# A chunked scan with a feed-forward layer: output sums of the middle blocks moved, two loads on another queue, the last product in another bank

## The chip, the cores and the metric

The kernel runs on one core of one Trainium2 chip. The metric is the device time of one execution in microseconds (us). The page of a profile calls the engines PE (TensorE, matmuls), PEld (its weight loads), DVE (VectorE), ACT (ScalarE), POOL (GpSimd) and SP (SyncE). A name with a q (ACTq, SPq) is the engine's instruction queue: DMA issues and waits, not arithmetic. L372 is line 372 of the kernel.

The kernel before has two levels of time, some 5 us apart, and which one a run takes changes from run to run. Runs of the upper level are called slow. Where a kernel's runs all lie close together they are all counted as fast, even if their clock is low.

## The reference, cut to what matters

```python
# x (4, 8, 768, 32), a (4, 8, 768), B and C (4, 8, 768, 16), float32
# a scan with decays over the sequence, per head
cum = np.cumsum(log_a, axis=-1)
L = np.exp(cum[:, :, :, None] - cum[:, :, None, :]) * causal
y_intra = (C B^T * L) @ x
y_inter = (C @ state) * exp(cum)
state = decay_full * state + sum(B x * decay_from_j)
# a feed-forward layer on its output: 3072 tokens of 256, hidden 768
h = np.maximum(np.maximum(y @ w1, y @ w2), y @ w3)
out = h @ w_out
```

(The einsums are abbreviated.) The kernel cuts the sequence into six chunks of 128 tokens (NC = 6) instead of 32, takes four batches and eight heads at once, and does the feed-forward products with seven block products instead of eight (that is why there are so many sums and quarters in it).

## The kernel before: the parts that matter here

Loads and their queue. Every load below is issued by SyncE (`nc.sync`):

```python
    def load(c, name):                         # L122: B, C or x of chunk c
        ...
        nc.sync.dma_start(out=t, in_=src[:, :, c * P:(c + 1) * P, :].rearrange(...))

    def decay_load(c, pairs=(0, 2)):           # L369: two loads of 1 MB, decays of chunk c
        L = decays(c) if 0 in pairs else Ls[c]
        for b in pairs:
            nc.sync.dma_start(out=L[:, b:b + 2]..., in_=cums[...].partition_broadcast(P))

    def last_load(c):                          # L377: eight small loads (32 KB each), "E"
        for h in range(NH):
            nc.sync.dma_start(out=E[h * N:(h + 1) * N], in_=rows[h].partition_broadcast(N))
```

One step of the feed-forward part. ScalarE's copy L653 opens a chain that frees the PSUM banks for TensorE: L653 on ScalarE, L654 to L656 on VectorE, then products of the next step.

```python
    def early(c, k):                           # L628 are the products
        products(c, k, [(1, A, 0), (6, A, 1), (5, B, 0), (7, B, 1)], True)
        ...
        nc.scalar.copy(out=eu[:, 0], in_=A[:, 0])                                      # L653
        nc.vector.tensor_tensor(out=eu[:, 1], in0=A[:, 1], in1=eu[:, 0], op=ALU.add)   # L654
        nc.vector.tensor_tensor(out=v, in0=B[:, 1], in1=eu[:, 1], op=ALU.add)          # L655
        nc.vector.tensor_tensor(out=t[:, 2], in0=B[:, 0], in1=v, op=ALU.add)           # L656

    def quarter_sums(o, t):                    # of the output; L745, L746, L747
        nc.vector.tensor_tensor(out=t[:, 0], in0=o[:, 1], in1=t[:, 1], op=ALU.add)
        nc.vector.tensor_tensor(out=t[:, 2], in0=o[:, 3], in1=t[:, 0], op=ALU.add)
        nc.vector.tensor_tensor(out=t[:, 3], in0=o[:, 2], in1=t[:, 2], op=ALU.add)
```

The loop interleaves, in block c, the feed-forward part of chunk c, the scan of chunk c + 1 and the output of chunk c - 1. Lists say what goes with which of nine steps: X and Y which piece (scores "s0", "s2", scan "y", output product "D"), P how many waiting VectorE instructions are popped at three points of a step. `flush()` issues the quarter sums that wait.

```python
    for c in range(1, NC):
        n = c + 1
        for k in range(NW):                    # nine steps
            early(c, k)
            ...                                # pieces of X; pops
            maximum = late(c, k)
            if n < NC and k == 0:
                loads(c + 2)                   # all loads of chunk c + 2
            ...
            pop(ps_[k][2])                     # score weightings (L491), sums of y (L553)
            flush()                            # quarter sums (L745 to L747)
            later[:0] = maximum
            ...
```

## Time and profile before

| | before |
|---|---|
| four runs, us | 297.81, 297.83, 302.54, 303.39 |
| profiled run (slow) | 302.34, span 300.6, mean granted TensorE clock 0.988 |
| TensorE busy | 94% of the span |
| waits that the change is aimed at | 7.3 us in all, counted in the prediction |

### The profile page before, as it was taken

The page shows a single profiled execution, that of the slowest core. Times are in us where ns is not written, and L with a number is a line of the kernel's source. Part 1 is how long each engine was busy: PE and PEld are TensorE (multiplying, and loading weights), DVE is VectorE, ACT ScalarE, POOL GpSimd, SP SyncE. Part 2 cuts the span into 40 slices and gives each one's busy share as a digit, 9 for nine tenths or more (in the row PEclk, how much of TensorE's full clock was granted, in tenths as well). Part 3 has the DMA queues.
Part 4 walks back from the last instruction along what each step waited for, and adds up shares of the span by engine and source line. Part 5 has one row for each costly group of instructions (what it writes and reads, how often), then busy time and mean ns, then how long its engine had stood idle before and what let it go on. Part 6 is the DMA issues. An engine that isn't in the chain of part 4 may idle for free.

```text
span 300.6 us, 5773 instructions
## 1 busy us (share of the span) xinstructions
PE 282.3 (94%) x2204; PEld 225.9 (75%) x2204; DVE 212.9 (71%) x427; ACT 119.5 (40%) x323; POOL 112.8 (38%) x132
## 2 busy tenths in 40 slices
PE   6789999989999999899999999999989999999994
PEld 4556445478887878688977878888878888988984
DVE  2763878957789467868577868676778676677681
ACT  2946487743756345424426242525220201011101
POOL 5252656477990917900005920003530303030300
PEclk9969999999999999999999999999999999999999
DMA  7979879969787039950007690001001001000103
GB/s 90 227 248 320 181 132 178 255 173 206 210 96 106 2 96 250 106 77 2 2 0 219 145 139 27 3 0 37 0 0 37 2 1 35 2 1 0 37 0 105
DMA packets 105035, 28.15 MB, mean 94 GB/s; under 512 B 75312, under 2 KB 101936, under 8 KB 105008
## 3 DMA queue, kind: packets, MB, share of 16 engines
q1 hardware_dynamic: 104560, 27.53, 45.7%
q8 instruction: 17, 0.28, 0.4%
q10 hardware_dynamic: 448, 0.26, 0.3%
q14 instruction: 10, 0.08, 0.1%
HBM read 24.54 MB, written 3.24 MB: 92 GB/s over the span
## 4 chain that ended last, share of the span: by engine, by line
PE 77%; DVE 12%; issue 3%; DMA 3%; SPq 2%; ACT 1%; POOL 0%; DVEq 0%; ACTq 0%; POOLq 0%
PE sumB L628 22%; PE sumA L628 17%; PE o L738 15%; PE up L578 8%; PE s L483 4%; PE y L519 3%; DMA raw_x<-in_x_dram 3%; PE o L814 3%; DVE L L491 2%; PE y L506 2%; PE up L570 2%; DVE m L673 2%; PE y L530 1%; DVE rb L670 1%; SPq L125 1%
## 5 line engine op out<-in xcount | busy, mean ns | idle before, releaser
L628 PE MATMUL sumA<-yT,w 128*128 128x256 f32 x180 | 55.5, 390 | 1.4 <-DVE h L669 1.4
L653 ACT COPY eu<-sumA 128x256 f32<-128x256 f32 x45 | 16.8, 373 | 87.6 <-PE sumA L628 80.0
L391 ACT ACTIVATE L<-L,ncums 128x128 f32<-128x128 f32 x160 | 50.2, 392 | 2.5 <-POOL L L384 2.5
L628 PE MATMUL sumB<-rb 128*128 128x256 f32 x180 | 46.2, 379 | 0.0
L628 PEld LDWEIGHTS sumB<-rb 128*128 128x128 f32 x180 | 34.2, 190 | 4.7
L628 PEld LDWEIGHTS sumA<-yT,w 128*128 128x128 f32 x180 | 29.8, 190 | 9.0 <-DVE h L669 2.6
L654 DVE TENSOR_TENSOR eu<-sumA,eu 128x256 f32<-128x256 f32 x45 | 18.9, 420 | 18.9 <-ACT eu L653 18.5
L491 DVE TENSOR_TENSOR L<-s,L 128x512 f32<-128x512 f32 x46 | 29.8, 680 | 1.1 <-PE s L483 0.7
L578 PE MATMUL up<-yT,w 128*128 128x512 f32 x64 | 29.1, 600 | 0.2 <-DVE w L188 0.2
L670 DVE TENSOR_TENSOR rb<-sumB,eu 128x512 f32<-128x512 f32 x30 | 20.7, 690 | 10.4 <-PE sumB L628 10.3
L628 PE MATMUL sumB<-yT,rb 128*128 128x256 f32 x90 | 27.5, 387 | 0.6 <-DVE m L656 0.6
L185 POOL TENSOR_TENSOR w_u<-w_u,w_r 128x512 uint32<-128x512 uint32 x12 | 15.3, 1274 | 31.9 <-DVE w_u L179 15.5
L628 PE MATMUL sumB<-rb,w 128*128 128x256 f32 x90 | 26.8, 379 | 0.0
L628 PE MATMUL sumA<-rb 128*128 128x256 f32 x90 | 26.8, 379 | 0.0
L384 POOL TENSOR_SCALAR_AFFINE_SELECT L<-L 128x1024 f32<-128x1024 f32 x20 | 24.1, 1235 | 0.0
L470 POOL TENSOR_TENSOR S<-S,old 128x256 f32<-128x256 f32 x4 | 2.9, 726 | 56.2 <-DVE S L462 56.1
L713 POOL TENSOR_TENSOR L<-h 128x256 f32<-128x256 f32 x5 | 3.6, 726 | 52.2 <-DVE h L673 40.1
L655 DVE TENSOR_TENSOR v<-sumB,eu 128x256 f32<-128x256 f32 x45 | 19.1, 425 | 5.0 <-DVE eu L654 0.5
L578 PEld LDWEIGHTS up<-yT,w 128*128 128x128 f32 x64 | 11.6, 190 | 14.7 <-issue 11.7
L738 PE MATMUL o<-wo,h 128*128 128x128 f32 x120 | 17.5, 279 | 4.9 <-DVE ob L747 4.9
L738 PEld LDWEIGHTS o<-wo,h 128*128 128x128 f32 x120 | 15.9, 191 | 7.9 <-issue 5.0
L670 DVE TENSOR_TENSOR m<-sumB,eu 128x512 f32<-128x512 f32 x15 | 10.3, 690 | 15.4 <-PE sumB L628 15.3
(141 smaller groups left out, 512.5 us busy)
## 6 DMA issues: line engine op xcount, KB each, us to landing
L<-cums SPq DMA_DIRECT2D x10, 1024.0 KB, 8.8
rb<-in_moe_w_dram SPq DMA_DIRECT2D x9, 512.0 KB, 7.6
raw_x<-in_x_dram SPq DMA_DIRECT2D x6, 512.0 KB, 7.8
out_dram<-ob SPq DMA_DIRECT2D x11, 256.0 KB, 2.2
raw_B<-in_B_dram SPq DMA_DIRECT2D x6, 256.0 KB, 4.5
raw_C<-in_C_dram SPq DMA_DIRECT2D x6, 256.0 KB, 6.5
rb<-in_moe_w_out_dram SPq DMA_DIRECT2D x3, 512.0 KB, 6.0
E<-cums SPq DMA_DIRECT2D x40, 32.0 KB, 4.4
```

What stands on the lines that cost most here:

```text
L185: nc.gpsimd.tensor_tensor(out=u, in0=u, in1=r, op=ALU.add)
L384: nc.gpsimd.affine_select(out=Ls[c][:, b], in_=Ls[c][:, b], pattern=[[0, NH], [1, P]], compare_op=ALU.is_ge, fill=MASKED, base=0, channel_ ...
L391: nc.scalar.activation(L[:, b, h], L[:, b, h], AF.Exp, bias=ncum[c][:, b * NH + h:b * NH + h + 1], scale=1.0)
L483: nc.tensor.matmul(out=s[:, i].rearrange("j g i -> j (g i)"), lhsT=st["BT"][rows, b], rhs=st["CT"][rows, b].rearrange("p g i -> p (g i)"), ...
L491: nc.vector.tensor_tensor(out=M, in0=s, in1=M, op=ALU.mult)
L578: nc.tensor.matmul(out=bank, lhsT=w_sb[i][:, k, f * P:(f + 1) * P], rhs=yT[0][:, k], start=(k == 0), stop=(k == KD - 1))
L628: nc.tensor.matmul(out=bank[:, half], lhsT=left(p, k), rhs=sides[c][p], start=(first and half == 0), stop=True, skip_group_check=True)
L653: nc.scalar.copy(out=eu[:, 0], in_=A[:, 0])
L654: nc.vector.tensor_tensor(out=eu[:, 1], in0=A[:, 1], in1=eu[:, 0], op=ALU.add)
L655: nc.vector.tensor_tensor(out=v, in0=B[:, 1], in1=eu[:, 1], op=ALU.add)
L670: nc.vector.tensor_tensor(out=t[:, 0:2], in0=B, in1=eu[:, 1:2].to_broadcast([P, 2, HB]), op=ALU.add)
L738: nc.tensor.matmul(out=o[:, PLACES[p]], lhsT=token_sums[c][p][:, f, u], rhs=wo_of(p)[:, f], start=(p == 1 and f == 0), stop=True, skip_gro ...
```

## The change

Its intent: give the quarter sums a whole step before the products that need them; spread the VectorE work of block 1; let the last product start without waiting for a bank; and take two loads of chunk 2 (x, and the second half of the decays) off SyncE's queue, issuing them from ScalarE somewhat nearer to their use. The diff, cut to its core:

```diff
# part 1, block 1: VectorE's instructions popped at other points
-    P1 = [..., (1, 1, 3), (1, 1, 0), (1, 0, 0), (9, 0, 0)]
+    P1 = [..., (1, 1, 2), (1, 1, 1), (1, 0, 2), (1, 0, 2)]
# parts 2 and 3, middle blocks: scores and y one step earlier, products and quarter sums later
-    X2 = ["t", "s0", "D", "D", "s2", "D", "y", "D", "D"]
+    X2 = ["t", "s0", "D", "s2", "D", "y", "D", "D", "D"]
-    P2 = [(1, 0, 1), (1, 1, 1), (1, 0, 2), (1, 0, 0), (1, 1, 1), (1, 0, 2), (1, 0, 2), (1, 0, 2), ...]
+    P2 = [(1, 0, 1), (1, 1, 3), (0, 0, 1), (1, 1, 2), (1, 0, 0), (1, 0, 0), (9, 0, 0), (1, 0, 0), ...]
-            flush()
+            if not (1 < c < NC - 1 and k == 2):
+                flush()
# part 4, the end: last product in its own bank, ScalarE's copy and store ahead of the last sum
-        token_products(c, 1, o, (4,))
+        o = att_bank([P, 4, P], "o")
+        token_products(c, 1, o, (4,), first=4)
# part 5, the queues
-            decay_load(2, (2,))                # both stood in SyncE's list before block 1
-            load(2, "x")
+    decay_load(2, (2,), nc.scalar)             # just before block 1
+            if c == 1 and k == 1:              # in block 1, step 1
+                load(2, "x", nc.scalar)
# [helpers with a queue as an argument, and the place of a sum in the last output: cut]
```

More of the change, by code (lines that the diff above doesn't have):

```diff
@@ L120, with load @@
     sources = {"B": (B, N), "C": (C, N), "x": (x, D)}
-    def load(c, name):
+    def load(c, name, eng=nc.sync):
         src, w = sources[name]
         t = blocks[c][name] = raw.tile([P, BH, w], FP32, tag="raw_" + name, name="raw_" + name)
-        nc.sync.dma_start(
+        eng.dma_start(
             out=t, in_=src[:, :, c * P:(c + 1) * P, :].rearrange("b h s n -> s (b h) n"))
@@ L367, with decay_load @@
     cums = dram.tile([BH, NC, P], FP32, name="cums")
-    def decay_load(c, pairs=(0, 2)):
+    def decay_load(c, pairs=(0, 2), eng=nc.sync):
         L = decays(c) if 0 in pairs else Ls[c]
         for b in pairs:
-            nc.sync.dma_start(
+            eng.dma_start(
                 out=L[:, b:b + 2].rearrange("j b h i -> j (b h) i"),
@@ L733, in flush, with token_products @@
             behind.pop(0)()
-    def token_products(c, u, o, which, fs=range(NQ)):
+    def token_products(c, u, o, which, fs=range(NQ), first=1):
         for p in which:
@@ L739, in token_products, with quarter_sums @@
                     out=o[:, PLACES[p]], lhsT=token_sums[c][p][:, f, u], rhs=wo_of(p)[:, f],
-                    start=(p == 1 and f == 0), stop=True, skip_group_check=True)
-    def quarter_sums(o, t):
-        nc.vector.tensor_tensor(out=t[:, 0], in0=o[:, 1], in1=t[:, 1], op=ALU.add)
-        nc.vector.tensor_tensor(out=t[:, 2], in0=o[:, 3], in1=t[:, 0], op=ALU.add)
+                    start=(p == first and f == 0), stop=True, skip_group_check=True)
+    def quarter_sums(o, t, w):
+        nc.vector.tensor_tensor(out=w, in0=o[:, 1], in1=t[:, 1], op=ALU.add)
+        nc.vector.tensor_tensor(out=t[:, 2], in0=o[:, 3], in1=w, op=ALU.add)
         nc.vector.tensor_tensor(out=t[:, 3], in0=o[:, 2], in1=t[:, 2], op=ALU.add)
@@ L750, in new_quarters @@
         if tag == "m":
-            ob = ffn.tile([P, 4, HB], FP32, tag="m", name="m")[:, 0:2]
+            ob = ffn.tile([P, 4, HB], FP32, tag="m", name="m")
         else:
@@ L773, in output_products @@
             nc.scalar.copy(out=t[:, 1], in_=o[:, 0])
-            behind.append(lambda: quarter_sums(o, t))
+            behind.append(lambda: quarter_sums(o, t, t[:, 0]))
         if 4 in which:
@@ L846, in last_output @@
         obs = [new_quarters(tag) for tag in ("ob", "m")]
-        for o, (ob, t) in zip(os, obs):
+        for o, (ob, t), place in zip(os, obs, (0, 4)):
             nc.scalar.copy(out=t[:, 1], in_=o[:, 0])
-            quarter_sums(o, t)
+            quarter_sums(o, t, t[:, place])
         flush()
@@ L854, in last_output @@
         token_products(c, 1, o, (2, 3))
-        nc.vector.tensor_tensor(out=t[:, 1], in0=o[:, 2], in1=t[:, 0], op=ALU.add)
-        token_products(c, 1, o, (4,))
-        nc.vector.tensor_tensor(out=t[:, 2], in0=o[:, 3], in1=t[:, 0], op=ALU.add)
+        nc.scalar.copy(out=t[:, 0], in_=o[:, 0])
+        nc.vector.tensor_tensor(out=t[:, 1], in0=o[:, 2], in1=t[:, 4], op=ALU.add)
+        nc.scalar.dma_start(out=rows[:, 2], in_=ob[:, 0])
+        o = att_bank([P, 4, P], "o")
+        token_products(c, 1, o, (4,), first=4)
+        nc.vector.tensor_tensor(out=t[:, 2], in0=o[:, 3], in1=t[:, 2], op=ALU.add)
         nc.sync.dma_start(out=rows[:, 3], in_=ob[:, 1])
-        nc.scalar.copy(out=t[:, 0], in_=o[:, 0])
-        nc.scalar.dma_start(out=rows[:, 2], in_=ob[:, 0])
     for b in range(2, NB):
@@ L1036 @@
     Y1 = ["", "", "D", "", "", "D", "", "D", ""]
-    P1 = [(1, 0, 0), (1, 0, 0), (1, 0, 1), (1, 1, 2), (1, 0, 0), (1, 1, 3), (1, 1, 0), (1, 0, 0),
-          (9, 0, 0)]
+    P1 = [(1, 0, 0), (1, 0, 0), (1, 0, 1), (1, 1, 2), (1, 0, 0), (1, 1, 2), (1, 1, 1), (1, 0, 2),
+          (1, 0, 2)]
     D1 = [(0, 0), (0, 0), (2, 0), (2, 0), (2, 0), (2, 0), (0, 2), (0, 1), (0, 2)]
     K1 = {0: (0, (0, 1)), 2: (0, (2, 3)), 4: (1, (0, 1)), 6: (1, (2, 3))}
-    X2 = ["t", "s0", "D", "D", "s2", "D", "y", "D", "D"]
+    X2 = ["t", "s0", "D", "s2", "D", "y", "D", "D", "D"]
     Y2 = ["D", "D", "", "", "", "", "", "", ""]
-    P2 = [(1, 0, 1), (1, 1, 1), (1, 0, 2), (1, 0, 0), (1, 1, 1), (1, 0, 2), (1, 0, 2), (1, 0, 2),
+    P2 = [(1, 0, 1), (1, 1, 3), (0, 0, 1), (1, 1, 2), (1, 0, 0), (1, 0, 0), (9, 0, 0), (1, 0, 0),
           (1, 0, 0)]
```

## The prediction

> **What bounds the kernel now.** I read the page first (shares by engine), then the waits of TensorE, then the timeline of single stretches, since the average says nothing about where a wait ends last. PE is matmul, DVE VectorE, ACT ScalarE, POOL GpSimd, SPq the queue of SyncE. The page's busy line and its chain of waits:
>
> ```profile
> PE 282.3 (94%) x2204; PEld 225.9 (75%) x2204; DVE 212.9 (71%) x427; ACT 119.5 (40%) x323; POOL 112.8 (38%) x132
> PE 77%; DVE 12%; issue 3%; DMA 3%; SPq 2%; ACT 1%; POOL 0%; DVEq 0%; ACTq 0%; POOLq 0%
> ```
>
> ```profile
> PE o L738 <- DVE ob L747: 4.9, 7, 1.2
> PE o L814 <- issue: 1.5, 1, 1.5
> PE sumA L628 <- DVE h L669: 1.4, 3, 0.7
> PE sumB L628 <- DVE m L656: 0.6, 3, 0.3
> PE o L738 <- DVE m L855: 0.4, 1, 0.4
> ```
>
> TensorE is the bound. No matmul is taken away by this change, so only TensorE's idle time can be won. The second fence shows its waits after the first 60 us that the change could touch: 4.9 us for the quarter sums (L747), 1.4 + 0.6 us for the stage sums (L669, L656), 0.4 us at the end. The sum is 7.3 us. A wait costs some 0.15 us more than it shows, because modelled matmul ends run past the next start (0.59 us shown at a pace of 0.43). The issue gap is dealt with below.
>
> VectorE is second. The loop has blocks 1 to 5 of nine steps each (0 to 8); block 3, say, does the feed-forward part of chunk 3, the scan of chunk 4 and the output of chunk 2; 2 to 4 are the middle blocks. There VectorE is full exactly where the waits are (block 3, steps 2 and 3; start, length, what):
>
> ```profile
> 168.11 0.42 DVE L654 TENSOR_TENSOR eu<-sumA,eu 128x256 f32<-128x256 f32 x1 [0.70 <-ACT eu L653]
> ...
> 169.44 1.68 DVE L673 TENSOR_TENSOR m<-m,rb 128x768 f32<-128x768 f32 x1
> 171.04 0.41 DVE L669 TENSOR_TENSOR h<-m,sumA 128x256 f32<-128x256 f32 x1
> 171.37 0.68 DVE L670 TENSOR_TENSOR rb<-sumB,eu 128x512 f32<-128x512 f32 x1
> 171.97 1.27 DVE L491 TENSOR_TENSOR L<-s,L 128x512 f32<-128x512 f32 x2
> 173.16 0.27 DVE L745 TENSOR_TENSOR ob<-o,ob 128x128 f32<-128x128 f32 x1
> 173.47 0.29 DVE L746 TENSOR_TENSOR ob<-o,ob 128x128 f32<-128x128 f32 x1
> 173.80 0.29 DVE L747 TENSOR_TENSOR ob<-o,ob 128x128 f32<-128x128 f32 x1
> 174.00 0.41 DVE L654 TENSOR_TENSOR eu<-sumA,eu 128x256 f32<-128x256 f32 x1
> ```
>
> ```profile
> 171.50 0.70 PE L628 MATMUL sumA<-yT,w 128*128 128x256 f32 x2 [0.39 <-DVE h L669]
> ...
> 174.23 0.91 PE L738 MATMUL o<-wo,h 128*128 128x128 f32 x6 [0.74 <-DVE ob L747]
> ```
>
> The reader is to see a queue in program order: the maximum (L673), then L669 which frees sumA, then L670, two score weightings (L491), then the three quarter sums, and TensorE waits at L669 and again at L747. From the start of L670 to the start of the products is 174.23 - 171.37 = 2.86 us; this figure is used below.
>
> **What the Trainium skill says.** PSUM — Partial Sum Buffer, section "PSUM bank collisions raise a hardware error": guard PSUM by bank, not by address, since two engines on one bank collide even at other columns. The trace agrees that waits are kept so: the last product writes quarter 3 and yet waits 0.39 us for L855, which reads quarter 2 of the same bank. SBUF — State Buffer, section "Who interferes with whom": a VectorE instruction with two SBUF inputs contends with a GpSimd instruction that reads SBUF. The trace agrees: L673 took 1.68 us under GpSimd's masks (4.95 us from 169.20) and 0.95 us elsewhere. DMA: Bandwidth & Descriptors, section "Issuing engines are not separate DMA queues": another issuing engine saves issue time only, and all transfers interleave on the same 16 DMA engines. The trace before has too few loads on ScalarE to show it. Runtime: NRT & Kernel Launch, section "Instruction fetch mechanics": instructions come by DMA in 16 KiB blocks. The trace fits: 17 packets, 0.28 MB, on an instruction queue, one of them under way at 61.7 to 63.2 us, just when TensorE stands for "issue" for 1.48 us.
>
> **Part 1: block 1 (weightings and y sums spread out).** Before, all four weightings of the second score group are popped by the end of step 5, and all four y sums (L553) in the last step, ahead of L669. Two waits come from this. (a) At 96.85 the second late product waits for L656. Its place is 95.82 + 0.53 = 96.35, so 0.50 is lost. With one weighting (0.68) after the stage's three sums, L654 starts at 94.97 (the stage's start 93.42 + the usual 1.55) instead of 95.31, L656 ends at 96.37, and about 0.42 us is won. (b) At 110.42 sumA waits for L669, which stands behind the maximum (107.64) and four sums to 110.04. The place without it is 109.53, so 0.89 is lost. With two sums one step earlier and two after L670, L669 can start 0.64 after its product began at 108.24, long before it is needed; the third sum is done by 110.77, and its product's place is 109.53 + 3 x 0.43 = 110.82. So 0.89 us is won. Together 1.3 us.
>
> **Part 2: middle blocks, first half of the output (three blocks).** Scores go from step 4 to step 3, the products that wait for the quarter sums from step 3 to step 4, and the flush of step 2 is left out, so the quarter sums are issued at the end of step 3. It looks as if they got a whole step of slack. But they again come behind L670 and two weightings (the new list pops two at the end of step 3), so the 2.86 us chain stands ahead of the same products, one step later. Take block 3: the four weightings in step 1 push L656 from 169.52 to 169.93, still in time. L669 is no longer behind L673, so step 3 starts at 170.94 instead of 171.50: 0.56 won. L673 now comes after L670 (171.75), still under the masks, and ends at 173.4. The stage sums of step 3 then run 173.35 to 174.75 instead of from 172.48, the late product waits to 174.81 (place 174.36), step 4 starts at 175.67, and L670 comes after the second maximum and one weighting, at 176.14. Plus 2.86 is 179.00 for the products, whose place is 177.40: a wait of 1.6 us in place of 0.9. They end at 181.08. Before, the same work (products and scores) was done at 180.50. So 0.55 us is lost. Block 2 has the same timing to the masks (they end 12.5 us after its step 1 begins in both): 0.55 lost. Block 4 has no masks; there the same count gives products ending at 226.90 against scores ending at 226.83: nothing. Sum: 1.1 to 1.2 us lost.
>
> **Part 3: middle blocks, second half.** y goes from step 6 to 5, and its sums and the state sum to step 6 (all popped at once). Before, one y sum (0.41) and the state sum (0.41) stand between L670 and the quarter sums of step 7. The real stall there is 153.25 - 151.56 - 0.86 = 0.83, again 0.83 one block later, and about 0.5 in the third. After: step 6 has 1.35 (stage) + 0.95 + 1.5 (four sums) + 0.4 + 0.65 = 4.85 us of VectorE against 4.4 of TensorE, a backlog that L654 of step 7 takes as a delay of some 0.3 us, within the slack of its late products. In step 7 L670 is followed by the quarter sums at once: 0.6 + 0.31 + 0.33 + 0.29 + 0.14 = 1.67 from L670's start, against 1.53 at which the products could start. About 0.14 is left. Won: 0.69 + 0.69 + 0.36 = 1.7 us.
>
> **Part 4: the end.** The last product gets another bank and need not wait for L855: it starts at 295.68 instead of 296.20, 0.52 won. ScalarE's copy (0.27) and its store come before the last sum instead of after it; before, ScalarE's store was issued 0.31 us after SyncE's (297.80 against 297.49). Together 0.8 us.
>
> **Part 5: the queues.** 1 MB of decays goes from SyncE at 64.28 to ScalarE at about 62.7, and x (0.5 MB) from 64.70 to about 71. No instruction after 16 us waits long for a load (the page's only sizeable DMA piece is the first x), so nothing is won directly. ScalarE pays the issues: 0.4 us for the decays, for x 0.5 to 3.5 us (the six x issues on SyncE: median 2.1). It is free from 70.86 to 74.72 there, so x is hidden at the median. I count 0. The instruction-fetch gap at 63.19 stays, because what fills the queues before 61.7 us is not moved.
>
> Sum: 1.3 - 1.15 + 1.7 + 0.8 = 2.65 us, 0.9%.
>
> **Rivals.** (i) The slack is real: if the quarter sums get out of the way in step 3, all of 0.9 + 0.9 + 1.4 us plus the 0.56 twice is won instead of 1.15 lost; total about 6.5 us, over 2%. For it: it is plainly what was meant. Against: the order of VectorE's queue and the two weightings popped just before the flush. (ii) VectorE becomes the bound: steps 3 (5.6 us of work against 4.2 of TensorE) and 6 are overfull, and if masks slow both maxima the loss of part 2 doubles and part 3 keeps only half: total near 0.5 us. (iii) The x issue holds ScalarE longer than its 3.85 us, or the added transfers lengthen the fetch gap: each up to 1.5 us lost. Nothing speaks for it but the longest issue of the decays, 5.2 us.
>
> **Range and chances.** Three runs before gave 297.81, 302.54 and 303.39, so there are two levels some 5 us apart, and the profiled run is of the upper one. I expect the same two levels 2.65 us lower, 295.2 and 300.0 to 300.7. I name 299.5, near the upper one, and the range 294.8 to 302.0 holds both levels and rival (ii). Like against like, 2% is 6 us: only rival (i) in full reaches it. Chance of faster 0.08, within 2% 0.88, slower 0.04.
>
> **What would show it.** In part 1 no wait of sumA for L669 at the seam of blocks 1 and 2. In part 2 waits of o for L747 of 1.2 to 1.7 us in step 4 of all three blocks; if these are gone, rival (i) is right and I misread VectorE's order. In part 3 waits under 0.2 us at step 8. In part 4 the last product straight behind the one before. In part 5 no longer idle time of DVE for the copy L653 around 75 us; if there is some, rival (iii) holds.

## More of the kernel before

What bounds the kernel is worked out in the prediction. One view that it does not show locates the two levels. It is a table of busy time by stretch (start and end in us, length, busy us of each engine with its count, the granted TensorE clock, the DMA share, GB/s), from the slow run that was profiled:

```profile
17.00:24.00 7.00, 6.30 (x73) 3.97 (x71) 3.56 (x8) 1.72 (x3) 2.52 (x2) 0.53 0.72 221
```

The clock is about half in this early stretch.

Just ahead of it TensorE waits for the first load of x:

```profile
PE A L451 <- DMA raw_x<-in_x_dram: 1.2, 1, 1.2
```

(That the late load causes the half clock is not tested.)

## The result, and the profile after

| | before | after |
|---|---|---|
| runs, us | 297.81, 297.83, 302.54, 303.39 | 304.39, 305.09, 305.43, 307.49 |
| median of four | 300.19 | 305.26 |
| ratio of fast runs, with its 95% interval | | 1.0272 (1.0200 to 1.0343) |

The changed kernel is slower, and lies above the predicted range. All ratios here are the mean time of one kernel's fast runs over that of the other's in the same rounds, so they are not quite the ratio of the medians beside them. The outputs of the changed kernel and of all experiments are correct.

The profiled run of the changed kernel is the one of 304.39 us. It has no early stretch at half clock, so it is to be compared with the fast level of before: 304.39 against 297.82 us is 6.6 us, or 2.2%. (Its other three runs have clocks of 0.972 to 0.977 against 0.988, so they probably have more half-clock time, which the 1.0272 includes; no trace of them exists.) The busy shares of the page and TensorE's waits after the first 60 us, which answer to the first two fences of the prediction:

```profile
PE 284.1 (94%) x2204; PEld 227.1 (75%) x2204; DVE 212.7 (70%) x427; ACT 119.5 (39%) x323; POOL 112.8 (37%) x132
```

```profile
PE sumA L628 <- DVE eu L654: 5.2, 2, 3.7
PE o L738 <- DVE ob L747: 4.5, 4, 1.4
PE sumB L628 <- DVE m L656: 0.7, 3, 0.4
```

The columns of the second are the sum of the wait, the times, and the longest. Three of the five waits shown before are gone: those for L669, the "issue" gap and the one for L855. The wait for L747 is almost as large as before, in fewer and longer pieces, as predicted. But at the top stands a wait that was not there: TensorE waits 5.2 us for L654, in two places. Follow it back. L654 on VectorE needs the copy L653 of ScalarE. Its waits in the same profile name a DMA:

```profile
ACT eu L653 <- DMA E<-cums: 9.1, 1, 9.1
ACT BT L406 <- PE o L814: 4.1, 1, 4.1
```

Neither copy reads anything of E. ScalarE's timeline from the start of block 1 shows what they are behind (start, length, instruction, and in brackets the idle time before it):

```profile
63.50 0.46 ACTq L372 DMA_DIRECT2D L<-cums  x1
64.05 0.58 ACT L406 COPY BT<-trB 128x512 f32<-128x512 f32 x1 [4.13 <-PE o L814]
...
70.00 0.37 ACT L653 COPY eu<-sumA 128x256 f32<-128x256 f32 x1 [2.30 <-PE sumA L628]
78.90 0.45 ACTq L125 DMA_DIRECT2D raw_x<-in_x_dram  x1
79.46 0.37 ACT L653 COPY eu<-sumA 128x256 f32<-128x256 f32 x1 [9.08 <-DMA E<-cums]
```

Right behind the two issues that were moved to it, ScalarE takes up work that has been due for long. From its copy's end at 70.37 to the issue at 78.90 it does nothing for 8.5 us; before the first issue, from 59.9 to 63.50, 3.6 us. The issues themselves last 0.46 and 0.45 us: what is long is the time before them. In the kernel before, the same copies waited for TensorE alone:

```profile
70.49 0.37 ACT L653 COPY eu<-sumA 128x256 f32<-128x256 f32 x1 [0.19 <-PE sumA L628]
74.72 0.37 ACT L653 COPY eu<-sumA 128x256 f32<-128x256 f32 x1 [3.85 <-PE sumA L628]
```

TensorE after:

```profile
65.42 0.70 PE L628 MATMUL sumA<-yT,w 128*128 128x256 f32 x2 [1.50 <-DVE eu L654]
66.50 0.90 PE L628 MATMUL sumB<-yT,rb 128*128 128x256 f32 x2 [0.38 <-DVE m L656]
67.20 1.06 PE L628 MATMUL sumB<-rb,w 128*128 128x256 f32 x2
...
80.34 1.14 PE L628 MATMUL sumA<-yT,w 128*128 128x256 f32 x2 [3.70 <-DVE eu L654]
```

The idle time shown is 1.50 + 0.38 + 3.70 = 5.6 us. And the pair of products at 67.20 takes 1.06 us, where later pairs of the same kind take 0.59: after each stop the clock is halved for a while. The stretches, after:

```profile
66.00:71.00 5.00, 4.62 (x14) 3.71 (x14) 2.84 (x6) 1.95 (x5) 3.02 (x6) 0.66 1.19 307
71.00:80.00 9.00, 5.64 (x27) 4.44 (x25) 2.60 (x6) 0.54 (x2) 8.84 (x15) 1.00 0.81 187
80.00:84.00 4.00, 3.65 (x8) 2.56 (x9) 2.83 (x6) 2.70 (x9) 3.84 (x7) 0.57 1.55 150
```

and before:

```profile
66.00:71.00 5.00, 5.00 (x27) 4.41 (x26) 3.44 (x8) 3.44 (x7) 2.70 (x4) 1.00 1.12 249
71.00:80.00 9.00, 9.00 (x42) 7.50 (x41) 6.85 (x13) 3.82 (x11) 8.77 (x15) 1.00 1.14 238
80.00:84.00 4.00, 4.00 (x31) 3.03 (x30) 3.17 (x6) 2.98 (x11) 3.92 (x6) 1.00 0.37 96
```

The clock's mean is 0.66 and 0.57 where it was 1.00 (third column from the end; then come the DMA share and GB/s), and in the middle row ScalarE is busy for 0.54 us of 9, TensorE for 5.64. The half-clock stretches run from 66.8 to 70.2 and from 80.5 to 83.9, 3.41 us each; half the clock over 2 x 3.41 us costs 3.4 us. The Trainium skill, TensorE: Matmul & The Clock Gate, section "Part 1: The HAM clock gate (the "warmup" mystery)", gives a window of 3413 ns and two states, half and full; the lengths agree.

To see what each part did, the traces can be cut at landmarks of TensorE's program. Start to start, in us; the column "block 1, first part" is from the first product of block 1 to the first scores of chunk 2 (the blocks are cut at their transposes):

| kernel | block 1, first part | to block 2 | block 2 | block 3 | block 4 to the last matmul | after it |
|---|---|---|---|---|---|---|
| before | 15.94 | 31.22 | 46.10 | 46.54 | 92.24 | 3.46 |
| after | 25.52 | 30.18 | 45.69 | 46.22 | 91.16 | 3.18 |
| difference | +9.58 | -1.04 | -0.41 | -0.32 | -1.08 | -0.28 |

All that the change was meant to win is there, 3.1 us after the first part of block 1. It is given back three times over in that first part.

### The profile page after: what moved, and what is told of

Same layout as the page of the kernel before. It is cut to its first block, busy times and chain, and to the rows that moved or that the text cites.

```text
span 302.7 us, 5767 instructions
## 1 busy us (share of the span) xinstructions
PE 284.1 (94%) x2204; PEld 227.1 (75%) x2204; DVE 212.7 (70%) x427; ACT 119.5 (39%) x323; POOL 112.8 (37%) x132
## 4 chain that ended last, share of the span: by engine, by line
PE 74%; DVE 13%; DMA 3%; SPq 2%; POOL 2%; issue 2%; ACT 1%; ACTq 0%; DVEq 0%; POOLq 0%
PE sumB L628 22%; PE sumA L628 16%; PE o L738 16%; PE up L578 5%; PE s L483 3%; DMA E<-cums 3%; DVE L L491 3%; PE y L519 2%; SPq L380 2%; PE o L814 2%; PE y L506 1%; PE spread L320 1%; PE up L570 1%; POOL w_u L185 1%; DVE m L673 1%
## 5 line engine op out<-in xcount | busy, mean ns | idle before, releaser
L628 PE MATMUL sumA<-yT,w 128*128 128x256 f32 x180 | 56.2, 394 | 5.2 <-DVE eu L654 5.2
L653 ACT COPY eu<-sumA 128x256 f32<-128x256 f32 x45 | 16.8, 373 | 81.7 <-PE sumA L628 66.3
L628 PEld LDWEIGHTS sumA<-yT,w 128*128 128x128 f32 x180 | 30.5, 192 | 12.2 <-DVE eu L654 6.3
L654 DVE TENSOR_TENSOR eu<-sumA,eu 128x256 f32<-128x256 f32 x45 | 18.9, 421 | 24.2 <-ACT eu L653 23.9
L491 DVE TENSOR_TENSOR L<-s,L 128x512 f32<-128x512 f32 x46 | 29.7, 681 | 0.3
L670 DVE TENSOR_TENSOR rb<-sumB,eu 128x512 f32<-128x512 f32 x30 | 20.7, 691 | 12.9 <-PE sumB L628 12.9
L628 PE MATMUL sumB<-yT,rb 128*128 128x256 f32 x90 | 28.5, 399 | 0.7 <-DVE m L656 0.7
L628 PE MATMUL sumB<-rb,w 128*128 128x256 f32 x90 | 27.7, 390 | 0.0
L628 PEld LDWEIGHTS sumB<-yT,rb 128*128 128x128 f32 x90 | 16.0, 192 | 6.8 <-DVE m L656 2.3
```

The lines of the kernel that those rows point to most:

```text
L491: nc.vector.tensor_tensor(out=M, in0=s, in1=M, op=ALU.mult)
L628: nc.tensor.matmul(out=bank[:, half], lhsT=left(p, k), rhs=sides[c][p], start=(first and half == 0), stop=True, skip_group_check=True)
L670: nc.vector.tensor_tensor(out=t[:, 0:2], in0=B, in1=eu[:, 1:2].to_broadcast([P, 2, HB]), op=ALU.add)
```

## The experiments

**The theory.** Why does an issue wait? The list of the compiled changed program, ScalarE's part, with the semaphores that the two issues wait for:

```
64:62 L372 DMACopy L<-cums 128x16x128 [waits DMAHW6_49]
72:70 L125 DMACopy raw_x<-in_x_dram 128x32x32 [waits DMAHW7_49,DMAHW3_49]
```

The program has eight completion semaphores for all DMA issues of SyncE and ScalarE together, DMAHW0 to DMAHW7, handed out in turn in program order. An issue waits until the earlier transfer with its semaphore has landed. (Compiled program and trace agree here: the last issues before the two moved ones with DMAHW6 and DMAHW3 are E loads, which land at 63.48 and 78.88 us.) For both moved loads the earlier user is one of the small E loads, queued on SyncE behind loads of 1 MB. SyncE's timeline after:

```profile
65.86 12.48 SPq L380 DMA_DIRECT2D E<-cums  x8
```

The chain of waits of the changed kernel (start, length, what) shows the hand-over, twice:

```profile
59.50 3.98 DMA E<-cums
63.48 0.02 issue
63.50 0.46 ACTq L372
...
74.37 4.51 DMA E<-cums
78.88 0.02 issue
78.90 0.45 ACTq L125
```

A load of E lands at 63.48 and the decays are issued at 63.50; another lands at 78.88 and x is issued at 78.90. Theory S, then: ScalarE is held by the semaphore that it shares with SyncE's queue. The rival R: a large load issued on ScalarE holds that engine whatever else the queues do, or its transfer at this time crowds out the others. And a question beside them: is the loss in part 5 alone?

**1. Part 5 alone.** The kernel before with only the queues changed.

```diff
 (before)
-            decay_load(2, (2,))
-            load(2, "x")
+    decay_load(2, (2,), nc.scalar)
+            if c == 1 and k == 1:
+                load(2, "x", nc.scalar)
```

> Only part 5 of the change (second half of chunk 2's decays and chunk 2's x issued by ScalarE), schedule and end as before. Theory S (each issue waits until the transfer that last used the same one of eight completion semaphores has landed, so ScalarE stands still behind SyncE's late loads): two holds of ScalarE of about 3.6 and 8.5 us at 60 to 79 us as in the changed kernel, TensorE idle some 5.6 us there and two half-clock windows of 3.4 us: 8 to 11 us slower than before (+2.7 to +3.7%). Rival Q (the loss comes from the new order of the middle blocks): within 1% of before.

Measured: median 308.51 us, ratio to before 1.0386 (1.0361 to 1.0410), a little more than was expected. The first part of block 1 takes 27.54 us, and TensorE waits 5.9 us for L654. ScalarE's two issues come at 63.87 and 79.39; the E loads had landed at 63.84 and 79.37. All its runs have clocks of 0.977 to 0.983. The loss is in part 5, and needs nothing of the others.

**2. The change without part 5.**

```diff
 (after)
+            decay_load(2, (2,))
+            load(2, "x")
-    decay_load(2, (2,), nc.scalar)
-            if c == 1 and k == 1:
-                load(2, "x", nc.scalar)
```

> The whole change except part 5: both loads stay on SyncE in their old places. Theory S with the sums of the prediction: parts 1 to 4 give 1.3 - 1.15 + 1.7 + 0.8, so 2 to 3 us faster than before (ratio 0.990 to 0.993). Rival Q: still over 1% slower than before. In the trace: waits of o for L747 of 1.1 to 1.5 us in step 4 of three blocks, none at step 8.

Measured: median 293.91 us, ratio 0.9884 (0.9867 to 0.9902). The first part of block 1 is back at 15.85 us, the other segments are those of the changed kernel within 0.05 us. So parts 1 to 4 win 1.16%, that is 0.0116 x 297.4 = 3.5 us, a little more than was expected (2 to 3). (The run that was profiled is a slow one; the other three are within 0.3 us of each other.)

**3. x earlier, before SyncE's loads of the next chunk.** The decays stay as changed. Now x's semaphore has an earlier user that has landed. S expects no hold for x; under R the same load on the same engine should still hold it.

```diff
 (after)
+            if c == 1 and k == 0:              # ahead of loads(3)
+                load(2, "x", nc.scalar)
-            if c == 1 and k == 1:
-                load(2, "x", nc.scalar)
```

> The whole change, but x of chunk 2 is issued by ScalarE one step earlier, ahead of chunk 3's loads in program order, so that its semaphore's last user is an early-landed load (63.8 us in the changed kernel); the decays stay as changed. Theory S: x issues within 1 us of ScalarE's copy before it (about 66 to 67 us), the 8.5 us hold is gone, the 3.6 us hold stays: -1.0 to +1.0% against before. Rival R (an issue on ScalarE cannot start while SyncE is working through its own string of issues, whatever the semaphores): x still issues only at about 78 us and the time is like the changed kernel's, +2.5% or more.

Measured: median 298.47 us, ratio 1.0047 (1.0030 to 1.0065). ScalarE's issue of x, and SyncE's group of E loads at the same time:

```profile
65.26 0.80 ACTq L125 DMA_DIRECT2D raw_x<-in_x_dram  x1
```

```profile
65.03 16.34 SPq L380 DMA_DIRECT2D E<-cums  x8
```

ScalarE passes in 0.80 us, while SyncE is taken up with its E loads for 16.34 us. The first half of R falls; the second, that x's transfer crowds out the others, falls with experiment 5, where x goes out at this time and costs 0.4 us (16.23 us for the first part of block 1, against 15.85). The other hold stays: the decays are issued at 62.60, after an E load that landed at 62.58, and TensorE waits 1.6 us for L654. The profiled run was the quickest (296.11 us, clock 1.0, no half-clock stretch at all after this wait); the other six have clocks of 0.981 to 0.994 and are 2 to 3 us longer.

**4. Both loads there.** S expects both issues to pass.

```diff
 (after)
-    decay_load(2, (2,), nc.scalar)
+            if c == 1 and k == 0:              # ahead of loads(3)
+                decay_load(2, (2,), nc.scalar)
+                load(2, "x", nc.scalar)
-            if c == 1 and k == 1:
-                load(2, "x", nc.scalar)
```

> The whole change, but both loads are issued by ScalarE in step 0 of block 1, ahead of chunk 3's loads in program order and after the earlier loads have landed (by 65.3 us in the changed kernel). Theory S: no hold of ScalarE over 1 us, time like e2_no_queues, ratio 0.985 to 0.995 against before. Rival R: held to about 78 us, +2.5% or more.

Measured: median 301.27 us, ratio 1.0136 (1.0117 to 1.0155). S missed this one. Its timeline of ScalarE:

```profile
64.01 0.40 ACTq L372 DMA_DIRECT2D L<-cums  x1
65.12 5.27 ACTq L125 DMA_DIRECT2D raw_x<-in_x_dram  x1
```

The semaphore did let x through, at 65.12, 0.02 us after its earlier user landed. But then the issue itself lasted 5.27 us, 1.1 us after a load of 1 MB on the same queue. TensorE stood for 5.1 us, and a half-clock stretch of 3.4 us followed. So there is a second way to hold ScalarE, which S does not contain. A theory for it, F: ScalarE's own queue is still full with the first load when the second comes.

**5. x early and alone on ScalarE.** It tests F: with the decays back on SyncE nothing is ahead of x on ScalarE's queue.

```diff
 (as 3, and)
+            decay_load(2, (2,))
-    decay_load(2, (2,), nc.scalar)
```

> As e3_x_before_loads, but the decays go back to SyncE, so that x is the only load on ScalarE's queue there. In e4_both_before_loads x waited for no semaphore of note and still took 5.27 us to issue, 1.1 us behind the decays on the same queue. Theory F (an issue is held while its own engine's queue is still full of an earlier transfer): x takes about 0.45 us, no idle gap of TensorE at 60 to 80 us, time like e2_no_queues (0.985 to 0.991). Rival G (the descriptors of x take ScalarE several us wherever SyncE is issuing too): 2 us or more, ratio over 0.993.

Measured: median 294.52 us, ratio 0.9892 (0.9872 to 0.9911).

```profile
64.09 0.44 ACTq L125 DMA_DIRECT2D raw_x<-in_x_dram  x1
```

The same load at the same point of the program takes 0.44 us in place of 5.27. That agrees with F; it does not show what fills. In experiment 3 x came 2.7 us after the decays and lasted 0.80 us, so the distance matters. The ratio is that of experiment 2 (0.9884): the move to ScalarE wins nothing even where it costs nothing.

**6. x as changed, decays on SyncE. 7. The decays as changed, x on SyncE.** They were to split the loss.

```diff
 (after)
+            decay_load(2, (2,))                # 6
-    decay_load(2, (2,), nc.scalar)
 (after)
+            load(2, "x")                       # 7
-            if c == 1 and k == 1:
-                load(2, "x", nc.scalar)
```

> The changed kernel with the decays back on SyncE and x where the change has it. Theory S: x's semaphore was last used by one of chunk 3's E loads, so ScalarE waits from about 70 us until that load lands, about 80 us; TensorE idle 3.5 us or more there and a half-clock window after it; ratio 1.005 to 1.02. If the hold needed the decays on the same queue: no gap, 0.985 to 0.991.

> The changed kernel with x back on SyncE and the decays where the change has them. Theory S: ScalarE held from the end of the y copies (60 us) to the landing of an E load of chunk 2 (63 to 64 us), TensorE idle about 2 us, with a half-clock window in some runs only; ratio 0.996 to 1.006. With e10_x_late_alone the two losses against e2_no_queues add up to the changed kernel's to within 2 us.

Measured: 305.29 us, ratio 1.0258 (1.0229 to 1.0287) for x; 299.70 us, ratio 1.0062 (1.0039 to 1.0085) for the decays. Both ratios lie above what was expected, and both holds are there. ScalarE with x alone, and with the decays alone:

```profile
79.17 0.46 ACTq L125 DMA_DIRECT2D raw_x<-in_x_dram  x1
79.74 0.37 ACT L653 COPY eu<-sumA 128x256 f32<-128x256 f32 x1 [8.53 <-DMA E<-cums]
```

```profile
65.83 0.45 ACTq L372 DMA_DIRECT2D L<-cums  x1
```

In both, the issue comes 0.02 us after an E load has landed (79.15 and 65.81). The first part of block 1 takes 21.30 us with x alone: 5.5 us over experiment 2, most of the whole. But the ratios can't be added up, as had been expected: against experiment 2 they lose 3.7% and 1.8%, together 5.5%, and the changed kernel loses 3.9%. Both profiled runs have the early half-clock stretch of the slow level (10.2 us and 6.8 us), some 5 us that have nothing to do with the holds, with all runs of each kernel at clocks of 0.977 to 0.983 and 0.987 to 0.994, so they are counted as fast only because they agree with each other. And in 7 the hold falls together with a gap of 1.45 us in which TensorE waits for nothing visible ("issue"), as in the slow run of before; L654 is not waited for, and the first part of block 1 takes 15.93 us, 0.1 over experiment 2. What the decays' hold costs by itself stays open; in experiment 3, where it was the only one, the first part of block 1 was 18.27 us, 2.4 us over experiment 2.

**8 to 10. Parts 1, 2 with 3, and 4 alone,** each on the kernel before, to size the other terms of the sum.

```diff
 8 (before): the new list P1
 9 (before): the new lists X2 and P2, and the flush of step 2 left out
10 (before): the new end
```

> Part 1 alone (weightings and y sums of block 1 spread out, all else as before). By the prediction 1.3 us faster (ratio 0.996); in the trace no wait of sumA for L669 at the seam of blocks 1 and 2 and none of sumB at step 6 of block 1. Rival: the 3.5 us won by parts 1 to 4 come mostly from elsewhere, then within 0.5 us of before.

> Parts 2 and 3 alone (order of the middle blocks, quarter sums of step 2 a step later). By the prediction 1.15 us lost in step 4 and 1.7 us won at step 8, so 0.55 us faster (ratio 0.998). Rival i (the slack is real): 5 us faster (0.983). Waits for L747 of 1.1 to 1.5 us in step 4 of three blocks, under 0.2 us at step 8.

> Part 4 alone (last product in its own bank, ScalarE's copy and store ahead of it). By the prediction 0.8 us faster (ratio 0.997); the last product follows the one before without a wait for L855's old sum.

| | fast runs' ratio | segments that moved, us |
|---|---|---|
| 8, block 1 | 0.9962 (0.9949 to 0.9976) | to block 2: 31.22 to 30.18 = -1.04 |
| 9, middle blocks | 0.9960 (0.9944 to 0.9976) | block 2 46.10 to 45.76, block 3 46.54 to 46.20, block 4 and on 92.24 to 91.80: -1.12 |
| 10, the end | 0.9971 (0.9959 to 0.9983) | block 4 and on 92.24 to 91.59, after the last matmul 3.46 to 3.18: -0.93 |

The three ratios sum to a win of 1.07%, and experiment 2 has 1.16%: the parts are additive. Of 17 runs of number 10, ten were slow, with medians that mean nothing; the ratios use fast runs.

**11. The quarter sums ahead of the weightings.** The prediction said that parts 2 and 3 give the quarter sums no slack because two score weightings (L491) are popped ahead of them. So: experiment 2 with one flush put ahead of that pop.

```diff
 (experiment 2)
+            if 1 < c < NC - 1 and k == 3:
+                flush()
             pop(ps_[k][2])
```

> The change without part 5, and the quarter sums of step 3 of the middle blocks issued before the two weightings popped there instead of behind them. If the failing slack of part 2 is VectorE's order, as the prediction says, the waits for L747 in step 4 fall from 1.4, 1.4 and 1.1 us to under 0.5 us each and the time to 6 to 7 us under before (ratio 0.976 to 0.981), 3 us under e2_no_queues. Rival: VectorE is simply full there (5.6 us of work against 4.2 us), so the wait moves to the next stage's sums and the time stays within 1 us of e2_no_queues (0.986 to 0.990).

Measured: median 291.05 us, ratio 0.9793 (0.9779 to 0.9807), 6.2 us under the fast level of before; faster than both kernels. That is what was expected, and its rival falls. VectorE's queue in block 3, steps 3 and 4, first in the changed kernel:

```profile
179.85 0.67 DVE L670 TENSOR_TENSOR m<-sumB,eu 128x512 f32<-128x512 f32 x1
180.45 1.27 DVE L491 TENSOR_TENSOR L<-s,L 128x512 f32<-128x512 f32 x2
181.65 0.27 DVE L745 TENSOR_TENSOR ob<-o,ob 128x128 f32<-128x128 f32 x1
...
182.28 0.29 DVE L747 TENSOR_TENSOR ob<-o,ob 128x128 f32<-128x128 f32 x1
```

then in this one:

```profile
168.26 0.67 DVE L670 TENSOR_TENSOR m<-sumB,eu 128x512 f32<-128x512 f32 x1
168.86 0.27 DVE L745 TENSOR_TENSOR ob<-o,ob 128x128 f32<-128x128 f32 x1
...
169.49 0.29 DVE L747 TENSOR_TENSOR ob<-o,ob 128x128 f32<-128x128 f32 x1
169.70 1.28 DVE L491 TENSOR_TENSOR L<-s,L 128x512 f32<-128x512 f32 x2
```

From the start of L670 to that of L747 it is 182.28 - 179.85 = 2.43 us in the first and 169.49 - 168.26 = 1.23 in the second: the two weightings, 1.2 us, stand behind instead of ahead. TensorE's waits and the page's busy line:

```profile
PE o L738 <- DVE ob L747: 1.0, 3, 0.6
```

```profile
PE 279.5 (97%) x2204; PEld 224.2 (78%) x2204; DVE 213.8 (74%) x427; ACT 119.7 (41%) x323; POOL 113.4 (39%) x132
```

The wait for L747 falls from 4.5 us to 1.0, each of blocks 2, 3 and 4 is 1.1 us shorter, and TensorE is busy for 97% of the span.

## Why the prediction was wrong, point by point

**The step that failed is part 5.** It priced an issue on ScalarE at its own duration (0.4 us for the decays, 0.5 to 3.5 us for x), found ScalarE free from 70.86 to 74.72, and wrote "I count 0". The missing term is the time before the issue: it waits for another transfer to land that has the same completion semaphore, here one on SyncE's queue. Nine pairs of landing and issue, in seven kernels, lie 0.02 to 0.03 us apart. On SyncE only other DMA issues stand behind such a wait. On ScalarE the copy L653 stands behind it, and behind that VectorE's sums and TensorE's products. In the changed kernel's trace the term comes to 5.6 us of visible idle time plus 3.4 us of half clock, 9.0 of the 9.6 us that the first part of block 1 is longer. (Of the rest, some is idle time that modelled matmul ends hide; that is argued, not shown.) The Trainium skill, DMA: Bandwidth & Descriptors, section "Anatomy of one DMA — SWDGE (gpsimd) path", says that the DMA engines do not wait on semaphores, and that any such wait is taken by the issuing sequencer before it dispatches. (The section describes transfers that GpSimd issues.) ScalarE's 8.5 us show the same for ScalarE; the prediction took from the same page only that issue time is small.

The failing rival (iii) had the right engine and place: it named a hold of ScalarE around 75 us and gave the view that would show it. But it rested on the length of issues and allowed 1.5 us each, and "slower" was given a chance of 0.04. The check that was missed needs no run: which transfer last had the semaphore of the moved issue, and when did its like land in the trace before? There SyncE's x load, the decays and the E loads around 65 to 83 us show that a load of that group lands late: its seven E issues from 74.43 span 9.02 us.

**"The instruction-fetch gap stays" was wrong as well.** The gap of 1.48 us is absent in the changed kernel's profile, and in the fast profiles of experiments 5 and 8 to 11. It is in the slow run of before and in experiment 7, both with the early half-clock stretch, but not in experiments 2 and 6, which have that stretch too. Nor was the fetch under way "just when" TensorE stood: among the packets of the trace it ends at 63.22 us, as the gap begins (63.19); in experiment 7 it ends at 64.32, and the gap begins at 64.14. In experiments 2 and 6 it ended some 2 us before these products began. So a late fetch fits, but no run tests it. The gap was a feature of the run that happened to be profiled, and not of the kernel.

**Part 1: right.** Predicted 1.3 us, measured 1.04; no wait for L669 is left at the seam of blocks 1 and 2, and none for L656 in step 6.

**Part 2: right in its mechanism, too dark in its sum.** Waits for L747 of 1.2 to 1.7 us were predicted in step 4 of all three blocks. They are 1.42, 1.42 and 1.10, and from the start of L670 to the products it is 182.62 - 179.85 = 2.77 us, where the prediction carried over 2.86. Experiment 11 shows that the cause was named rightly: without the two weightings ahead, the waits in step 4 are 0.22, 0.22 and under 0.1. With part 3 the middle blocks were to win 1.7 - 1.15 = 0.55; they won about 1.1 to 1.2. One term that was too large is the late product's wait in step 3, predicted at 0.45 and measured at 0.2 (in block 3 it starts 0.75 us after the product before it, 178.35 - 177.60, where 0.53 is the pace). Counted from the start of block 3, scores and products are done 0.47 us later than before (184.74 - 162.12 against 180.51 - 158.36); 0.55 was predicted.

**Part 3: right as to the waits,** those of step 8 are gone. Its size was not measured by a run of its own; in block 3 it comes to 0.47 + 0.32 = 0.79 us, where 0.69 was predicted.

**Part 4: right.** Predicted 0.8 us, measured 0.93. The last product follows the one before directly; in the changed kernel:

```profile
297.99 0.83 PE L738 MATMUL o<-wo,L 128*128 128x128 f32 x6
298.66 0.83 PE L738 MATMUL o<-wo_sums,h 128*128 128x128 f32 x6
```

**The sum.** Parts 1 to 4 were to win 2.65 us and win 3.5 (experiment 2), which is inside 2%. Rival (i), slack that is real, was rightly refused for this change; experiment 11 has it made true by one more line, and lands at the 6.2 us that rival (i) was given (6.5). Rival (ii), VectorE as the bound, did not come: its share is 70%, and the wait for L747 in the second halves is gone.

**Left open.** What the hold of the decays costs alone; what in ScalarE's queue makes the second issue of experiment 4 last 5.27 us; and what makes the first load of x land late in some runs, which sets the level of a run.

## What to carry to other kernels

Before moving a DMA issue to an engine that has other work, ask what the issue will wait for: in a program whose transfers share a few completion semaphores, it can wait for an older transfer of another queue, and then everything behind it on that engine waits too. Here no engine waited long for the moved loads, and the move won nothing even where it cost nothing (experiment 5). When an instruction is to get slack, read the order of the queue that it stands in: here one line that put three short sums ahead of two long ones was worth as much as all the rest of the change.

## What the Trainium skill lacked or had wrong

- DMA: Bandwidth & Descriptors, section "Issuing engines are not separate DMA queues": it weighs only the saved issue time, "usually small". It lacks the price on the other side, of which the page has only the sentence on the issuing sequencer cited above. ScalarE stood 8.5 us before an issue of 0.45 us, because of a completion semaphore shared with SyncE's transfers, and the change as a whole lost 2.7% (part 5 alone: 3.9%).
- The same page has nothing on an issue that itself lasts long behind another on its queue: 5.27 us when 1.1 us behind a load of 1 MB, 0.80 us when 2.7 us behind one, 0.44 us alone. Perfetto Trace Analysis lists the stages of an issue, but has no figure for such a hold either.
- TensorE: Matmul & The Clock Gate, section "Part 1: The HAM clock gate (the "warmup" mystery)": the table of the two states puts half clock down to at least one idle window of some 3.4 us (further down, the page also names frequent short idle times, without a length). Here the clock halved for 3.41 us after shown idle times of 1.50 and 0.38 us, 0.7 us apart; in the 3.41 us before it halved (63.39 to 66.80), TensorE was busy for 1.53 us. After a wait of 1.6 us in experiment 3 the profiled run had no such stretch.
- Runtime: NRT & Kernel Launch, section "Instruction fetch mechanics": fetches are called mostly hidden. TensorE stood 1.48 us (before, slow run) and 1.45 us (experiment 7) from within 0.2 us of the end of an instruction fetch; in the other eleven profiles no such gap shows. That the fetch is the cause is not shown.
